# First batch of a fused attention and MLP kernel: lambda spread as three 16-bit rows ahead of q's transposes, alpha1 around pooled k, alpha2 multiplied behind the transposes of u

## The chip, the cores and the metric

The kernel runs on one core of one Trainium2 chip. The metric is the device time of one execution in microseconds (us); the kernel before was timed three times. Its engines are TensorE (PE in the profile; PEld is its weight load), VectorE (DVE), ScalarE (ACT), GpSimd (POOL) and SyncE (SP). Loads and stores are DMA transfers, issued here from the queues of GpSimd, SyncE and ScalarE.

## The reference

Two stages over 8 batches of 576 tokens with 8 heads of 64. First attention with k and v averaged over groups of 8 tokens, so 72 pooled tokens; then a residual MLP with affine vectors:

```python
k_p = k.reshape(B, H, Sp, pool, D).mean(axis=3)
v_p = v.reshape(B, H, Sp, pool, D).mean(axis=3)
scores = scale * np.matmul(q, k_p.transpose(0, 1, 3, 2))
attn = softmax(scores)                       # written out, with + 1e-09
x = attn @ v_p                               # heads side by side: 576 x 512

a1 = alpha1 * x + beta1
tok = np.einsum('ts,bsd->btd', w_tok, a1)    # mixes tokens
u = x + lam * tok
a2 = alpha2 * u + beta2
ch = np.maximum(a2 @ w_ch1, 0.0) @ w_ch2     # 512 -> 2048 -> 512
out = u + lam * ch
```

`lam`, `alpha1` and `alpha2` are vectors of 512 columns.

## The kernel before, in words

**Tiling.** Tokens lie on the 128 partitions, five chunks of them to a batch; the fifth has 64 tokens and is joined with that of the neighbouring batch. Chunks are collected in blocks of four, and the MLP runs on one block of 512 tokens at a time. Block n is computed while the attention of batch n+1 runs between its matmuls. The first batch has no block to hide in: its attention and mix stand alone at the start, and this is the part that is changed.

**Order.** Nothing is scheduled by a planner there: each engine does its instructions in the order in which the Python code issues them (the calls from line 993 on). From block 0 on, the steps are sorted by a due time written beside each (`attention`, line 1076, and the loop at 1127), and are then issued in that order. An engine that waits holds everything behind it. DMA loads are issued in the same order on their engine's queue; those from GpSimd take some 0.6 to 0.9 us of GpSimd each. [...]

**The start.** `keep_warm` (788) runs matmuls on a tile of zeros until q is there. `att_F` (575) transposes q on TensorE, two calls for four heads; `cast_rem` (351) and `att_Frem` (603) do the same for the 64 tokens at the end. `spread_lam` (488) copies the row of lambda to all partitions by a matmul of a row of ones with it, in fp32, and ScalarE evicts it to `lam_bc`. `double_k` (618) repeats a quarter of k on VectorE, for `att_K` (624), which pools k with matmuls and evicts it twice, on ScalarE and on VectorE. `spread_al1` (494) spreads half of alpha1 by an fp32 matmul and multiplies it with `lam_bc` to `lamal_bc`. `att_S` (673) computes the scores of a head and their exponentials, `first_V` (651) pools v, `att_AV` (733) multiplies and normalises, and `att_X` and `rest_X` (761, 754) multiply with `lamal_bc` to `xs`, the moving operand of the mix. PSUM for all this comes from one pool of six banks, in turn.

**The mix.** `setup_wtok` (509) transposes w_tok, `setup_rowsum` (522) sums its rows for beta1 (`bias_row`, 469, is the row that they multiply). `mix_T` (794) computes the mix of one chunk, adds x on VectorE to `u`, and for batch 0 multiplies with `al2_bc`, alpha2 on all partitions, to the 16-bit `u_bf`: on GpSimd for chunks 0 and 2, on VectorE for 1 and 3. `al2_bc` is loaded by `load_al2` (484), 256 KB on SyncE's queue. `mix_uT` (813) transposes `u_bf` on TensorE for block 0, and ScalarE copies the result to `u_fm`, the MLP's moving operand. In later blocks alpha2 is inside w1 (`scale_w1`, 550) and DMA does the transposes.

**Batch 1, beside block 0.** Its q and k are loaded at the start from GpSimd's queue (lines 995 to 998), the w1 pieces 1 and 2 and v and w2 later (1047, 1056, 1060, 1064). `sum_k` (368) adds rows of k on GpSimd before `att_K` pools them; `cast_rem` on GpSimd makes `rem_q` and `rem_k` between the two halves. Both must be done when TensorE comes to `att_K(1, 0)`.

Of the kernel before, what the change touches and what calls it, by code (L numbers as in the profile page):

```python
# [14 lines left out]
P = 128  # L15
# [173 lines left out]
def direct(  # L189
# [199 lines left out]
    al2_bc = const.tile([P, DM], FP, tag="al2_bc", name="al2_bc")  # L389
    b2row = const.tile([8, P], FP, tag="b2row", name="b2row")  # L390

    vecs = const.tile([65, 3, DM], FP, tag="vecs", name="vecs")
# [59 lines left out]
            kpT_pool.append(t)  # L452
            kp_pool.append(const.tile([P, 4, SPG], BF, tag=f"kp_{i}", name=f"kp_{i}"))
    for i in range(2):
        t = const.tile([SPG, 4, S + 64], F16, tag=f"ET_{i}", name=f"ET_{i}")
        nc.vector.memset(t[:, :, S:], 1.0)
        ET_pool.append(t)
    xs_pool = [const.tile([P, 5, DM], BF, tag=f"xs_{i}", name=f"xs_{i}") for i in range(2)]
    nc.vector.memset(xs_pool[1][0:64, 4, :], 0.0)
    nc.vector.memset(pool_v[:, 64:], 0.0)  # L460
    nc.vector.memset(pool_vr, 0.0)
    nc.vector.memset(vr16, 0.0)
# [12 lines left out]
    wtT = const.tile([P, 6, 640], BF, tag="wtT", name="wtT")  # L475
    ones_lo = const.tile([P, P], BF, tag="ones_lo", name="ones_lo")

    def more_constants():
        nc.vector.memset(ones_bf, 1.0)
        nc.vector.memset(ones_lo[0:64], 1.0)  # L480
        nc.vector.memset(ones_lo[64:128], 0.0)
        nc.vector.memset(wtT[:, :, S:640], 0.0)

    def load_al2(behind):
        behind.memset(al2_bc[:, 0:1], 0.0)
        nc.sync.dma_start(out=al2_bc, in_=moe_alpha2.unsqueeze(0).to_broadcast((P, DM)))

    def spread_lam():

        ps = gp("ps_bc")  # L490
        nc.tensor.matmul(out=ps, lhsT=ones_row, rhs=vecs[0:1, 0])
        nc.scalar.copy(out=lam_bc, in_=ps)

    def spread_al1(half):

        ps = gp("ps_bc")[:, 0:256]
        cols = slice(256 * half, 256 * half + 256)
        nc.tensor.matmul(out=ps, lhsT=ones_row, rhs=vecs[0:1, 2, cols])
        nc.vector.tensor_tensor(out=lamal_bc[:, cols], in0=lam_bc[:, cols], in1=ps, op=ALU.mult)

    def setup_vectors():
        ps = gp("ps_vec")
# [115 lines left out]
    def double_k(u):  # L618

        nc.vector.tensor_copy(out=st1[0]["k"][u][:, :, 4], in_=st1[0]["k"][u][:, :, 0])  # L620
        if u == 0:
            cast_rem_k(nc.vector)

    def att_K(b, u, copy):

# [159 lines left out]
            }  # L785
        return key, st2[key]

    def keep_warm(count):

        ps = psB.tile([P, DM], FP, tag="ch", bufs=2, name="ps_warm")  # L790
        for _ in range(count):
            nc.tensor.matmul(out=ps, lhsT=warm[:, 0:P], rhs=warm)  # L792

    def mix_T(b, c, eng=nc.vector):
# [13 lines left out]
        if b:  # L808
            nc.scalar.copy(out=s["u_bf"], in_=s["u"])  # L809
        else:  # L810
            eng.tensor_tensor(out=s["u_bf"], in0=s["u"], in1=al2_bc, op=ALU.mult)

    def mix_uT(key):
        s = st2[key]
        i = where[key]
        blk, at = i // 4, i % 4
        if blk not in u_fm:
            u_fm[blk] = work.tile([P, 4, 512], BF, tag="u_fm", bufs=3, name="u_fm")
        if blk:
            nc.sync.dma_start_transpose(out=u_fm[blk][:, :, 128 * at:128 * at + 128],  # L820
                                        in_=s["u_bf"])
            return
        ps_uT = gp("ps_uT").bitcast(BF)
        for cc in range(4):
            nc.tensor.transpose(out=ps_uT[0:P, 128 * cc:128 * cc + 128],  # L825
                                in_=s["u_bf"][:, 128 * cc:128 * cc + 128], identity=identity_bf)
        nc.scalar.copy(out=u_fm[blk][:, :, at // 2, 128 * (at % 2):128 * (at % 2) + 128],
                       in_=ps_uT[:, 0:512].rearrange("p (c t) -> p c t", t=128))


    H4 = {}
# [78 lines left out]
    def weight_sum(i, g):  # L910
        lo, hi = w2l[g], w2l[g + 2]
        if "T1" not in wino:
            for t, tag in ((1, "w2_2"), (3, "w2_3")):
                wino[f"T{t}"] = const.tile([P, 8, HALF], BF, tag=tag, name="w2_t")
            wino["T2"] = [work.tile([P, 4, HALF], BF, tag="q_bf", bufs=4, name="w2_t2")
                          for _ in range(2)]
            wino["S2"] = [const.tile([P, 4, HALF], BF, tag=tag, name="h_s")
                          for tag in ("early", "al2_bc")]
# [75 lines left out]
    load_w1(0)  # L994
    load_q_bf(1, 0)
    load_q_bf(1, 1)
    for u in range(2):
        load_k(1, u, queue=nc.gpsimd)
    keep_warm(13)
    att_F(0, 0)  # L1000
    att_F(0, 1)
    cast_rem(0, nc.vector)
    more_constants()
    keep_warm(1)
    att_Frem(0, nc.scalar.copy)
    keep_warm(1)
    spread_lam()
    double_k(0)
    att_K(0, 0, None)
    spread_al1(0)  # L1010
    bias_row(0)
    att_S(0, 0)
    att_S(0, 1)
    first_V(0, 0)
    att_S(0, 2)
    double_k(1)
    att_AV(0, 0)
# [7 lines left out]
    att_AV(0, 3)  # L1025
    att_X(0, 2, 4, nc.gpsimd, False)
    rest_X(0, 0, 4, nc.gpsimd)
    att_S(0, 4)
    spread_al1(1)
    late_copy(nc.scalar.copy)  # L1030
    first_V(0, 1)
    load_al2(nc.vector)
    att_S(0, 5)
    att_AV(0, 4)
    att_S(0, 6)
# [8 lines left out]
    setup_wtok(2, nc.scalar.copy)  # L1044
    setup_rowsum(0)
    rest_X(0, 4, 6, nc.gpsimd)
    load_w1(1)
    setup_wtok(3, nc.scalar.copy)
    setup_rowsum(1)
    setup_wtok(4, nc.scalar.copy)  # L1050
    att_X(0, 6, 8)
    bias_row(1)
    mix_T(0, 0, nc.gpsimd)
    setup_vectors()
    setup_rowsum(2)
# [71 lines left out]
    for n in range(NBLK):  # L1127
# [51 lines left out]
                for m in range(4):  # L1179
                    todo.append((27.2 if m < 2 else 29.2, lambda m=m: store(n, m)))  # L1180
        if n == 0:
            todo.append((6.2, lambda: setup_rowsum(4)))
# [68 lines left out]
```

## Time and profile before

| | |
|---|---|
| median of 3 runs | 332.91 us (332.65 to 333.45) |
| the profiled execution | 332.3 us, its span 330.6 |
| TensorE busy | 324.9 us, 98% of the span |
| VectorE, ScalarE, GpSimd | 235.5, 175.5, 95.6 us |
| TensorE starts | 1.39 us |
| q's first transposes in the chain | 7.04 us |
| pooled k of batch 0, first half | 9.09 to 9.77 us |
| first mix matmul | 21.19 us |
| first halves of the MLP end | 29.54 us |
| pooled k of batch 1, first half | 35.36 to 35.52 us |

The page gives busy times per engine. The chain of waits follows the last instruction back to what released it, or to the instruction before it on its engine; read forwards, it says at each moment what the end of the program hung on. A matmul in it that is longer than its like hides a wait. A line of the timeline holds the start, the length, the engine, line, operation and tile, and in brackets how long the engine had been idle and what ended that. Landing times are from the start of a transfer's issue until its data is there.

### The profile page before, as it was taken

Reading aid. Unit: us, or ns where it says so; the run is one execution under the profiler, and the core shown is the slowest. Engines: PE = TensorE matmul, PEld = TensorE weight load, DVE = VectorE, ACT = ScalarE, POOL = GpSimd, SP = SyncE. Lnnn points to the kernel's source line nnn. Section 1 sums busy time; section 2 is a strip of 40 time slices with the busy share of each in tenths; the row PEclk is TensorE's granted clock in tenths of the full one; section 3 lists DMA queues with packets and bytes.
Section 4 is the critical chain, followed back from the end, with each engine's and each line's share of the span. In section 5 each row is a group of like instructions: output and inputs, shape, how many; then the busy total and the mean of one; then the engine's idle time right before and its main releaser. Section 6 shows DMA issues by size and latency. Waiting matters only on the chain.

```text
span 330.6 us, 6522 instructions
## 1 busy us (share of the span) xinstructions
PE 324.9 (98%) x2528; PEld 208.9 (63%) x2528; DVE 235.5 (71%) x490; ACT 175.5 (53%) x322; POOL 95.6 (29%) x110
## 2 busy tenths in 40 slices
PE   8999999999999999999999999999999999999995
PEld 3667764455545576656775677557755866586584
DVE  6674389999589969776967796878688783265263
ACT  2775989458323852387128812782268225803710
POOL 8769738301256011700290028102610200000000
PEclk9999999999999999999999999999999999999999
DMA  8999999959894982499549934995340044003003
GB/s 119 193 219 270 268 210 249 207 145 124 165 255 68 221 203 59 76 227 165 164 119 201 171 125 89 207 195 157 65 136 2 0 65 143 2 0 129 2 32 97
DMA packets 66618, 45.83 MB, mean 139 GB/s; under 512 B 34541, under 2 KB 57205, under 8 KB 66586
## 3 DMA queue, kind: packets, MB, share of 16 engines
q1 hardware_dynamic: 52236, 32.67, 42.6%
q0 software_dynamic: 13824, 12.40, 22.9%
q8 instruction: 20, 0.33, 0.4%
q10 hardware_dynamic: 526, 0.34, 0.3%
q14 instruction: 12, 0.10, 0.1%
HBM read 38.30 MB, written 9.44 MB: 144 GB/s over the span
## 4 chain that ended last, share of the span: by engine, by line
PE 98%; DVE 1%; issue 0%; ACT 0%
PE ps_h L849 38%; PE ps_w L972 26%; PE ps_tok L801 12%; PE ps_ch L869 8%; PE ps_av L743 3%; PE ps_s L700 2%; PE ps_warm L792 2%; PE ps_kp L632 1%; PE ps_r L707 1%; PE ps_av L747 1%; PE ps_q L589 1%; PE ps_sc L680 0%; PE ps_rs L528 0%; PE ps_w L516 0%; PE ps_uT L825 0%; PE ps_v L659 0%
## 5 line engine op out<-in xcount | busy, mean ns | idle before, releaser
L849 PE MATMUL ps_h<-u_fm,w 128*128 128x512 bf16 (+2 forms) x608 | 133.7, 369 | 0.2 <-DVE bias_cols L852 0.2
L856 ACT ACTIVATE H<-ps_h,bias_cols 128x512 bf16<-128x512 f32 x144 | 98.1, 688 | 56.5 <-PE ps_h L849 55.5
L849 PEld LDWEIGHTS <-w 128*128 128x128 bf16 x608 | 65.8, 114 | 49.7 <-issue 2.2
L972 PEld LDWEIGHTS <-H 128*128 128x128 bf16 x560 | 53.4, 98 | 10.9 <-DVE u_sb L990 1.2
L809 ACT CAST u_bf<-u_sb 128x512 bf16<-128x512 f32 x32 | 19.8, 618 | 70.0 <-issue 39.9
L972 PE MATMUL ps_w<-w_l,H 128*128 128x256 bf16 x448 | 53.6, 273 | 0.0
L990 DVE TENSOR_TENSOR u_sb<-u_sb,ps_w 128x512 f32<-128x512 f32 x54 | 36.3, 682 | 17.0 <-PE ps_w L972 17.0
L765 POOL TENSOR_TENSOR xs<-x_tm,lamal_bc 128x512 bf16<-128x512 f32 x12 | 15.9, 1330 | 108.8 <-DVE x_tm L751 108.6
L801 PE MATMUL ps_tok<-xs,wtT 128*128 128x512 bf16 (+3 forms) x200 | 44.9, 381 | 0.1
L805 DVE TENSOR_TENSOR u_sb<-x_tm,ps_tok 128x512 f32<-128x512 f32 (+1 forms) x40 | 27.3, 683 | 9.9 <-PE ps_tok L801 9.9
L751 DVE TENSOR_TENSOR x_tm<-ps_av,recs 128x320 f32<-128x320 f32 x64 | 31.5, 492 | 2.6
L729 ACT ACTIVATE ET<-ps_s 72x512 f16<-72x512 f32 x56 | 32.3, 591 | 0.0
L801 PEld LDWEIGHTS <-wtT 128*128 128x128 bf16 (+3 forms) x200 | 17.4, 100 | 16.2 <-issue 1.1
L749 DVE RECIPROCAL recs<-ps_av 128x5 f32<-128x5 f32 x64 | 12.1, 188 | 16.7 <-PE ps_av L747 16.6
L670 DVE TENSOR_TENSOR v_u<-v_u 72x1024 f32<-72x1024 f32 (+1 forms) x24 | 22.7, 948 | 0.2
L972 PE MATMUL ps_w<-w_t,h_s 128*128 128x256 bf16 x168 | 22.6, 273 | 0.0
L869 PEld LDWEIGHTS <-H 128*128 128x128 bf16 x128 | 11.9, 98 | 13.7 <-issue 0.4
L372 POOL TENSOR_TENSOR k_raw<-k_raw 128x512 f32<-128x512 f32 x14 | 18.7, 1338 | 1.2 <-PE ps_ch L869 0.7
L972 PEld LDWEIGHTS <-h_s 128*128 128x128 bf16 x168 | 16.4, 98 | 4.1
L941 DVE TENSOR_TENSOR H<-H,H 128x1024 bf16<-128x1024 bf16 x14 | 9.7, 690 | 12.8 <-ACT H L856 12.7
L374 POOL TENSOR_TENSOR k_bf<-k_raw 128x512 bf16<-128x512 f32 x14 | 18.5, 1318 | 1.1
L743 PEld LDWEIGHTS <-ET 72*128 72x128 f16 x256 | 14.0, 97 | 6.0 <-DVE vp L664 0.3
(153 smaller groups left out, 369.3 us busy)
## 6 DMA issues: line engine op xcount, KB each, us to landing
out_dram<-u_sb SPq DMA_DIRECT2D x29, 256.0 KB
k_raw<-in_k_dram SPq DMA_DIRECT2D x12, 512.0 KB
v_u<-in_v_dram SPq DMA_DIRECT2D x12, 512.0 KB
q_bf<-in_q_dram POOLq DMA_DIRECT2D x16, 256.0 KB, 7.4
w<-in_moe_w_ch_dram POOLq DMA_DIRECT2D x6, 512.0 KB, 12.9
out_dram<-u_sb SPq DMA_DIRECT2D x11, 128.0 KB
w<-in_moe_w_ch_dram POOLq DMA_DIRECT2D x1, 1024.0 KB, 14.3
k_raw<-in_k_dram POOLq DMA_DIRECT2D x2, 512.0 KB, 16.7
```

The source lines that it names most:

```text
L670: nc.vector.tensor_tensor(out=out, in0=t[:, :, 0:width], in1=t[:, :, width:2 * width], op=ALU.add)
L729: nc.scalar.activation(out=o, in_=i, func=AF.Exp, bias=0.0, scale=0.125)
L743: nc.tensor.matmul(out=av[:, odd + c, :], lhsT=ET[:, m0:m0 + 128], rhs=vp1[:, h % 4, :])
L751: nc.vector.tensor_tensor(out=x[:, 1 - odd:6 - odd, dd:dd + D], in0=av[:, :, 0:64], in1=rec.unsqueeze(2).to_broadcast((P, 5, D)), op=ALU.mult)
L801: nc.tensor.matmul(out=ps_tok[p0:p1], lhsT=wtT[0:kk, at, P * c:P * c + p1 - p0], rhs=xs_pool[i][0:kk, sc, :], start=(sc == 0), stop=(sc == 4))
L805: nc.vector.tensor_tensor(out=s["u"][p0:p1, :], in0=x[p0:p1, 1 + c if c < 4 else 5 - 5 * i, :], in1=ps_tok[p0:p1, 0:DM], op=ALU.add)
L809: nc.scalar.copy(out=s["u_bf"], in_=s["u"])
L849: nc.tensor.matmul(out=ps_h[:, t0:t1 + one], lhsT=w1_of(cc, j), rhs=rhs, start=(cc == 0), stop=(cc == 3))
L856: nc.scalar.activation(out=H4[n, j // 4][:, j % 4, :], in_=ps_h, func=AF.Relu, bias=bias_cols[:, j:j + 1], scale=1.0)
L869: nc.tensor.matmul(out=ps, lhsT=H_of(n, j)[:, 128 * m:128 * m + 128], rhs=(w2l if n else w2)[j // 4][:, j % 4, :], start=(j == 0), stop=(j ...
L972: nc.tensor.matmul(out=ps, lhsT=stat(j), rhs=moving(j), stop=(j == 7), start=(first and (pp == 0 or alone) and j == 0), skip_group_check=True)
L990: nc.vector.tensor_tensor(out=o, in0=o, in1=banks[key, "both"], op=ALU.add)
```

## The change

- `keep_warm` takes a width. The 13 matmuls of 512 columns become 14 of 64 and 8 of 512; the two single ones among q's transposes go.
- Lambda is split on VectorE into three bf16 rows that add up to it (a copy, the rest, a copy of that, the rest again), written into the first rows of `xs_pool[0]`, and spread by three bf16 matmuls ahead of q's transposes. Its eviction comes after the first eviction of pooled k on ScalarE.
- Alpha1's first half is spread ahead of pooled k, its second half right behind it, where it stood behind head 4's scores. Both VectorE products follow the second eviction of pooled k.
- `load_al2` and `al2_bc` go. For batch 0, ScalarE casts `u` to `u_bf`, and VectorE multiplies with alpha2, per partition, as it evicts the transposes.
- VectorE's memsets are put elsewhere: ones_bf before lambda's rows, ET behind `double_k`, the others of `more_constants` behind the alpha1 products, `vr16` behind head 3. `cast_rem_k` stands ahead of `double_k(0)`, `bias_row(0)` behind the first `first_V`.
- `load_w1(1)` is issued ahead of batch 1's k loads on GpSimd's queue. `setup_rowsum(4)` moves from block 0's due times to the end of the first MLP halves, and the first two `mix_uT` each move ahead by one step.

```diff
+    nc.vector.memset(ones_bf, 1.0)
+    rest = const.tile([1, DM], FP, tag="h_s", name="lam_rest")
+    parts = xs_pool[0][0:1, 0:3]
+    nc.vector.tensor_copy(out=parts[:, 0], in_=vecs[0:1, 0])
+    nc.vector.tensor_tensor(out=rest, in0=vecs[0:1, 0], in1=parts[:, 0], op=ALU.subtract)
+    nc.vector.tensor_copy(out=parts[:, 1], in_=rest)
+    nc.vector.tensor_tensor(out=parts[:, 2], in0=rest, in1=parts[:, 1], op=ALU.subtract)
...
+    def fill_ends():
+        for t in ET_pool:
+            nc.vector.memset(t[:, :, S:], 1.0)
+
     def more_constants():
-        nc.vector.memset(ones_bf, 1.0)
+        nc.vector.memset(xs_pool[1][0:64, 4, :], 0.0)
...
-    def load_al2(behind):
-        behind.memset(al2_bc[:, 0:1], 0.0)
-        nc.sync.dma_start(out=al2_bc, in_=moe_alpha2.unsqueeze(0).to_broadcast((P, DM)))
-
     def spread_lam():
         ps = gp("ps_bc")
-        nc.tensor.matmul(out=ps, lhsT=ones_row, rhs=vecs[0:1, 0])
-        nc.scalar.copy(out=lam_bc, in_=ps)
+        for part in range(3):
+            nc.tensor.matmul(out=ps, lhsT=ones_bf[0:1], rhs=xs_pool[0][0:1, part],
+                             start=(part == 0), stop=(part == 2))
+        def finish():
+            nc.scalar.copy(out=lam_bc, in_=ps)
+        return finish
...
+    def cast_u(b, c):
+        s = chunk_of(b, c)[1]
+        nc.scalar.copy(out=s["u_bf"], in_=s["u"])
...
         if b:
-            nc.scalar.copy(out=s["u_bf"], in_=s["u"])
-        else:
-            eng.tensor_tensor(out=s["u_bf"], in0=s["u"], in1=al2_bc, op=ALU.mult)
+            cast_u(b, c)
...
-        nc.scalar.copy(out=u_fm[blk][:, :, at // 2, 128 * (at % 2):128 * (at % 2) + 128],
-                       in_=ps_uT[:, 0:512].rearrange("p (c t) -> p c t", t=128))
+        nc.vector.tensor_tensor(
+            out=u_fm[0][:, :, at // 2, 128 * (at % 2):128 * (at % 2) + 128],
+            in0=ps_uT[:, 0:512].rearrange("p (c t) -> p c t", t=128),
+            in1=al2_cols.unsqueeze(2).to_broadcast((P, 4, 128)), op=ALU.mult)
...
     load_q_bf(1, 1)
+    load_w1(1)
     for u in range(2):
         load_k(1, u, queue=nc.gpsimd)
-    keep_warm(13)
+    keep_warm(14, 64)
+    keep_warm(8)
+    lam_copy = spread_lam()
     att_F(0, 0)
     att_F(0, 1)
     cast_rem(0, nc.vector)
-    more_constants()
-    keep_warm(1)
-    att_Frem(0, nc.scalar.copy)
-    keep_warm(1)
-    spread_lam()
-    double_k(0)
-    att_K(0, 0, None)
-    spread_al1(0)
-    bias_row(0)
+    cast_rem_k(nc.vector)
+    att_Frem(0, nc.scalar.copy)
+    al1_copies = [spread_al1(0)]
+    double_k(0)
+    fill_ends()
+    att_K(0, 0, None)
+    lam_copy()
+    al1_copies.append(spread_al1(1))
+    for copy in al1_copies:
+        copy()
+    more_constants()
     att_S(0, 0)
     att_S(0, 1)
     first_V(0, 0)
+    bias_row(0)
...
-    spread_al1(1)
     late_copy(nc.scalar.copy)
     first_V(0, 1)
-    load_al2(nc.vector)
...
-    load_w1(1)
...
-    mix_T(0, 0, nc.gpsimd)
+    mix_T(0, 0)
     setup_vectors()
+    cast_u(0, 0)
     setup_rowsum(2)
     load_w1(2)
     mix_T(0, 1)
+    mix_uT((0, 0))
+    cast_u(0, 1)
     setup_rowsum(3)
-    mix_T(0, 2, nc.gpsimd)
+    mix_T(0, 2)
     load_v32(1)
-    mix_uT((0, 0))
     mix_uT((0, 1))
+    cast_u(0, 2)
     mix_T(0, 3)
+    cast_u(0, 3)
...
     mlp_A(0, 3, 0, 256)
+    setup_rowsum(4)
     for j in range(4):
         mlp_A(0, j, 256, 512)
```

More of the change, by code (lines that the diff above doesn't have):

```diff
@@ L388, in direct @@
     lamal_bc = const.tile([P, DM], FP, tag="lamal_bc", name="lamal_bc")
-    al2_bc = const.tile([P, DM], FP, tag="al2_bc", name="al2_bc")
     b2row = const.tile([8, P], FP, tag="b2row", name="b2row")
@@ L454, in direct @@
     for i in range(2):
-        t = const.tile([SPG, 4, S + 64], F16, tag=f"ET_{i}", name=f"ET_{i}")
-        nc.vector.memset(t[:, :, S:], 1.0)
-        ET_pool.append(t)
+        ET_pool.append(const.tile([SPG, 4, S + 64], F16, tag=f"ET_{i}", name=f"ET_{i}"))
     xs_pool = [const.tile([P, 5, DM], BF, tag=f"xs_{i}", name=f"xs_{i}") for i in range(2)]
-    nc.vector.memset(xs_pool[1][0:64, 4, :], 0.0)
     nc.vector.memset(pool_v[:, 64:], 0.0)
     nc.vector.memset(pool_vr, 0.0)
-    nc.vector.memset(vr16, 0.0)
+    nc.vector.memset(ones_bf, 1.0)
[5 more added lines that the diff above has]
+    nc.vector.tensor_tensor(out=parts[:, 2], in0=rest, in1=parts[:, 1], op=ALU.subtract)
     nc.vector.tensor_scalar(out=pool_v[:, 0:64], in0=pool_main, scalar1=8.0, scalar2=None,
@@ L498, in spread_al1, with finish @@
         nc.tensor.matmul(out=ps, lhsT=ones_row, rhs=vecs[0:1, 2, cols])
-        nc.vector.tensor_tensor(out=lamal_bc[:, cols], in0=lam_bc[:, cols], in1=ps, op=ALU.mult)
+        def finish():
+            nc.vector.tensor_tensor(out=lamal_bc[:, cols], in0=lam_bc[:, cols], in1=ps,
+                                    op=ALU.mult)
+        return finish
     def setup_vectors():
@@ L620, in double_k @@
         nc.vector.tensor_copy(out=st1[0]["k"][u][:, :, 4], in_=st1[0]["k"][u][:, :, 0])
-        if u == 0:
-            cast_rem_k(nc.vector)
     def att_K(b, u, copy):
@@ L786, in chunk_of, with keep_warm, mix_T @@
         return key, st2[key]
-    def keep_warm(count):
-        ps = psB.tile([P, DM], FP, tag="ch", bufs=2, name="ps_warm")
+    def keep_warm(count, n=DM):
+        ps = psB.tile([P, DM], FP, tag="ch", bufs=2, name="ps_warm")[:, 0:n]
         for _ in range(count):
-            nc.tensor.matmul(out=ps, lhsT=warm[:, 0:P], rhs=warm)
-    def mix_T(b, c, eng=nc.vector):
+            nc.tensor.matmul(out=ps, lhsT=warm[:, 0:P], rhs=warm[:, 0:n])
+    def cast_u(b, c):
+        s = chunk_of(b, c)[1]
+        nc.scalar.copy(out=s["u_bf"], in_=s["u"])
+    def mix_T(b, c):
         key, s = chunk_of(b, c)
@@ L917, in weight_sum @@
             wino["S2"] = [const.tile([P, 4, HALF], BF, tag=tag, name="h_s")
-                          for tag in ("early", "al2_bc")]
+                          for tag in ("early", "h_s")]
             wino["S3"] = [const.tile([P, 4, HALF], BF, tag="lam_bc", name="h_s"),
@@ L1027, in direct @@
     rest_X(0, 0, 4, nc.gpsimd)
+    nc.vector.memset(vr16, 0.0)
     att_S(0, 4)
-    spread_al1(1)
     late_copy(nc.scalar.copy)
     first_V(0, 1)
-    load_al2(nc.vector)
     att_S(0, 5)
@@ L1181, in direct @@
         if n == 0:
-            todo.append((6.2, lambda: setup_rowsum(4)))
             todo.append((8.3, setup_wtok_odd))
```

## The prediction

> **What bounds the kernel now.** I read the busy table of the page first, then the chain of waits in order of time over the first 80 us, then POOL's timeline, and last the landing times of single transfers. The busy table says that TensorE is the bound; its idle time is 5.7 us of 330.6.
>
> ```profile
> PE 324.9 (98%) x2528; PEld 208.9 (63%) x2528; DVE 235.5 (71%) x490; ACT 175.5 (53%) x322; POOL 95.6 (29%) x110
> ```
>
> So time is won only by taking work off TensorE's own stream, or by shortening one of the few places where it waits, and it is kept only if nothing further down that stream waits for something else. In the chain (start, length, engine, tile, line) the places that the change touches are these:
>
> ```profile
> 1.39 5.66 PE ps_warm L792 x13
> ...
> 8.04 1.05 PE ps_bc L491 x2
> ...
> 9.79 0.40 ACT kpT L648
> ...
> 10.21 0.47 DVE kpT L648
> ...
> 15.31 0.62 PE ps_bc L498 x2
> ...
> 35.36 0.12 PE ps_kp L632 x4
> 35.48 0.04 PE ps_kp L638 x2
> ```
>
> Here are lambda's spread (1.05 us on TensorE), the wait of the first scores for two evictions of pooled k, the second half of alpha1 (0.62), and, 20 us later, batch 1's pooled k, which needs GpSimd's sums. POOL's timeline shows those sums and the loads in front of them:
>
> ```profile
> 12.55 0.76 POOL L280 DMA_DIRECT2D k_raw<-in_k_dram  x1 [0.85 <-PE ps_sc L680]
> 14.24 0.75 POOL L280 DMA_DIRECT2D k_raw<-in_k_dram  x1 [0.93 <-PE ps_kp L638]
> ...
> 30.12 1.33 POOL L372 TENSOR_TENSOR k_raw<-k_raw 128x512 f32<-128x512 f32 x1
> 31.52 1.27 POOL L374 TENSOR_TENSOR k_bf<-k_raw 128x512 bf16<-128x512 f32 x1
> 32.74 0.40 POOL L357 CAST rem_q<-rem_raw 128x256 bf16<-128x256 f32 x1
> 33.10 0.72 POOL L360 TENSOR_TENSOR rem_k<-rem_raw 128x256 bf16<-128x256 f32 x1
> ```
>
> From the first sum to the end of rem_k is 33.82 - 30.12 = 3.70 us, and TensorE uses rem_k at 35.48: 1.66 us of slack. The load that the first sum reads was issued at 12.55 and took
>
> ```profile
> DMA to landing us min/median/max: 16.7/16.7/16.7
> ```
>
> so it landed at 29.25, already after q's second half for batch 1 (issued 10.9, 16.8 to landing: 27.7). The loads of GpSimd's queue land one behind the other in the order of their issue: k's second half at 30.8, then w1's second piece, issued at 21.30, with
>
> ```profile
> DMA to landing us min/median/max: 12.0/12.0/12.0
> ```
>
> at 33.3. That is 2.46 us behind its forerunner; the third piece follows at 35.9, 2.6 later.
>
> **The start, up to q's transposes.** Removed are 13 wide warm-up matmuls, 5.66 us from 1.39, that is 0.427 each. In come 14 of 64 columns, 8 wide ones and lambda's three 16-bit rows. The eleven wide ones at 0.427 are 4.70. A 64-column matmul is not in the trace at this early pace; pooled k's 64-column ones take 0.47/16 = 0.029 later, where a wide one takes 0.22, so 0.06 at the half pace. The other end is the early weight load of 0.15. I take 0.06, the nearer kind: 14 x 0.06 + 4.70 = 5.5, the same as before; with 0.15 it is 1.2 later, and TensorE passes the gate below at 35.6 for 35.48, 0.1 slower. VectorE must have the third row ready by then: a copy and a subtraction, twice, on one row. The bias row (1x512) took 0.68, a 256-wide cast 0.31, a 128-wide one 0.21, so a 512-wide cast about 0.5, the chain 2.4 us. With the ET, xs and vr16 memsets moved away (0.55 + 0.27 + 0.27, the first of them into VectorE's wait for pooled k near 8.3) it starts at 3.7 and ends near 6.1, while the third row is wanted at 6.4. [...] So q's transposes start where they did, about 7.0, and pool_v on VectorE, which ended at 6.14, a little later, with rem_q near 6.5 to 7.0: cost nothing as long as rem_q is there at 7.4.
>
> **From there to the first scores.** Gone are two wide matmuls (0.44) and lambda's 1.05; alpha1's first half (0.62) moves ahead of pooled k. Pooled k ended at 9.77. Now k's landing (2.27 + 5.5 = 7.77) and its doubling (0.23) allow a start near 8.05, and with 0.57 + 0.10 it ends at 8.72: 1.05 earlier. Alpha1's second half now follows it (0.62), under the 0.40 + 0.47 of the two evictions. Lambda's copy (0.58) is behind the first eviction on ScalarE, so the first exponential waits for it, to 9.75. Second half of the first scores: 9.69 instead of 10.73.
>
> **To the mix.** VectorE becomes the limit: after the eviction it has both alpha1 products (0.42 each, from 9.77), the late memsets (about 0.85) and then vp's cast, which ends at 11.9 instead of 12.63. The bias row's 0.68 now stands between that cast and k's second doubling, so the second q copy, which gates the scores of head 4, gains only 0.23 (14.55 for 14.78). But 0.62 of alpha1 is gone behind head 4, and the next vp ends at 16.4 instead of 17.28: 0.9 us. Landing times allow it: q's second half 13.25, v's 14.7, w_tok 17.4, all ahead of their new uses. [...]
>
> **The mix.** ScalarE's four copies of transposed u (0.53 to 0.58) become VectorE products, priced at 0.68 as the like product with PSUM at line 875; two VectorE and two GpSimd products (0.69 to 0.77, 1.26) become ScalarE casts at 0.62 each. Per chunk the path is 0.69 + 0.62 in place of 0.69 + 1.26, and the 0.17 that the transposes waited for GpSimd goes. Against that the first MLP matmul waits about 0.1 for its product, and the second halves 0.25 for the last one, hidden partly by the moved row sum (0.15). Sum at the second halves: 0.95; with the row sum gone from 34.77, 1.1 us ahead when TensorE comes to batch 1's pooled k, at 34.3 instead of 35.36.
>
> **Where it goes.** There the queue order counts. w1's second piece now stands ahead of both k loads in GpSimd's queue, so k's first half lands 2.46 later, at 31.7, less what the removed alpha2 load gives back. That load is 256 KB on SP's queue; the queue view from 20 to 23.7 shows SP's and ScalarE's packets at 21.1% of the engines' time, 0.78 us. At most that comes back, at least nothing. The row nearest to it says little: w1's first piece, under whose transfer it lay, took 23.68 - 18.45 = 5.23, and two later halves 2.46 + 2.6 = 5.06, so 0.17. I take 0.3, near that row. [...]
>
> So k lands at 31.4, GpSimd starts at 31.45, ends rem_k at 35.15, and TensorE passes at 35.2, having stood for 0.8 us. Before, it passed at 35.48. The gain is 0.3 us, between 0.75 and nothing. The second half follows w2's issue (0.57) and two sums (1.3 each) and is ready at 38.4, ahead of its use at 39.2. v lands at 39.8 or earlier, as before, since the queue up to it holds the same loads; w2's loads stay behind it. Nothing later is touched, and TensorE is full from there.
>
> The profiled execution took 332.3, the median of the three runs is 332.91, 0.6 above it. 332.3 - 0.3 = 332.0, and on the scale of the median 332.6.
>
> **The rivals.** *The gain is kept.* If k's first half lands by 30.5 (or GpSimd's four steps take less than their 3.70), TensorE never stands, and 1.1 comes through: 331.8. For it: 98% TensorE, and the alpha2 load's removal. Against it: 2.46 of landing distance is three times what that removal can return.
>
> *The sums come later than I say.* Should w1's piece need more than 2.76 us in its new place, where the remainder rows share the engines (41% of SP's share from 23.7 to 25.6), TensorE passes later than before; with 1 us more than that, 333.6. For it: q's halves in that stretch took 1.9 and 2.1, and 1.3 earlier in the queue. Against it: the remainder rows are over when k passes now, and total traffic falls.
>
> *The slow start lasts longer: slower.* The early wide matmuls step at 0.427, the later ones at 0.22, although the granted clock prints 1.00 throughout; the pace changes near 6.9. If 14 narrow matmuls and three one-row ones do not count as work, it changes later. From 7.0 to the first scores there are about 2.7 us of TensorE work that would double, less 0.4 of waiting that hides it: TensorE is 2.3 later, of which the 1.1 of lead absorbs part, so it passes the gate at 36.7 for 35.48, 1.2 slower: 334.1. It decides from 1.1 us of delay on. Against it: TensorE has no gap from 1.39 on, and lambda's one-row matmuls at 8.04 did not bring the slow pace back. [...]
>
> **How the numbers follow.** The gate at k: 0.62. Gain kept: 0.14. Sums later: 0.12. Slow start: 0.12. A measurement here tells about 0.3%, 1.0 us, from no change. The kept gain is only just over that: with the gate's best end, faster is 0.16. The slow start and half of the late sums: slower 0.17. Same: 0.67. The range runs from 331.7, the kept gain, to 333.9, close to the slow start.
>
> **What would show it.** Right: q's transposes start within 0.2 us of 7.0; the first scores about 1 us earlier; the first mix matmul about 0.9 earlier than 21.19; k's first half lands near 31.4; GpSimd's first sum waits for that load; and TensorE has a gap of 0.5 to 1 us at batch 1's pooled k near 34.4, which is not there now. Wrong: no gap there, or a first sum near 30.1, or q's transposes at the slow pace (over 0.1 us each).

## The result and the profile after

The changed kernel takes 335.13 us (median of 17 executions, 333.76 to 337.04) against 332.9 before; the ratio is 1.0076 with a 95% interval of 1.0056 to 1.0096. It is slower by 2.2 us, and outside the forecast range (331.7 to 333.9). The executions are not spread evenly: 3 lie at 333.8 to 334.1, 7 at 334.9 to 335.3, 2 at 336.0 and 5 at 337.0. This spread is taken up below; where another kernel's executions fall into groups I give the groups, since the ratios leave out those more than 1.5% above the fastest of their kernel.

The profiled execution is one of the slowest group: 337.0 us, span 334.9. Its busy row still has TensorE at 98%, but 4.5 us more of it than before:

```profile
PE 329.4 (98%) x2536; PEld 213.6 (64%) x2536; DVE 238.6 (71%) x495; ACT 175.9 (53%) x322; POOL 93.5 (28%) x108
```

The chain of waits in order of time (start, length, engine, tile, line), at the places that answer to those shown of before:

```profile
1.39 4.34 PE ps_warm L804 x22
5.73 1.39 PE ps_bc L495 x3
7.12 0.97 PE ps_q L603 x8
...
8.30 1.15 PE ps_bc L507 x2
9.44 0.97 PE ps_kp L644 x16
...
10.50 1.15 PE ps_bc L507 x2
...
23.02 0.22 PE ps_av L755 x4
...
25.63 1.24 PE ps_tok L817 x5
...
34.17 1.92 PE ps_h L865 x16
...
39.62 0.12 PE ps_kp L644 x4
```

q's transposes start at 7.12, where the forecast had 7.0. But their eight take 0.97 us, 0.121 each, where they took 0.45 before. Pooled k takes 0.97 for 0.57, and half of alpha1 1.15 for 0.62. I call the slower pace half pace, the faster one full pace. TensorE does everything at half pace until about 23.5: at 23.02 four of `att_AV`'s matmuls still take 0.22 (0.15 at full pace), and the mix that follows has its old 1.24. The first mix is at 25.63 instead of 21.19, and from there nothing is lost or won: 8.54 us to the second halves of the MLP for 8.56 before, and 39.62 for 35.36 at batch 1's pooled k. The 4.3 us of difference in the span (334.9 for 330.6) are all there at the first mix.

This time the granted clock is no help. It prints 1.00 in every stretch of the first 40 us, also where a transpose takes 0.121 for the 0.056 of before; the half pace is read from the length of like instructions.

POOL's timeline (start, length, line, operation, idle time before it and what ended that), at the loads and sums of batch 1:

```profile
13.67 0.76 POOL L280 DMA_DIRECT2D k_raw<-in_k_dram  x1 [0.64 <-DVE wtT L489]
17.10 0.75 POOL L280 DMA_DIRECT2D k_raw<-in_k_dram  x1 [2.67 <-DVE x_tm L763]
...
29.70 1.26 POOL L372 TENSOR_TENSOR k_raw<-k_raw 128x512 f32<-128x512 f32 x1 [1.86 <-DMA k_raw<-in_k_dram]
...
34.58 0.73 POOL L360 TENSOR_TENSOR rem_k<-rem_raw 128x256 bf16<-128x256 f32 x1 [1.93 <-DMA rem_raw<-in_k_dram]
```

The sums wait for k's landing, as forecast, though k lands near 29.6 here and not near 31.4, with the remainder rows loaded later (rem_k waits 1.93 for them). rem_k is done at 35.31, 4.3 us before TensorE comes. The gap forecast at batch 1's pooled k does not exist in this execution: the gate was opened long before.

VectorE's timeline at the start shows two things that matter below: the row chain of lambda ends at 5.75, as forecast (6.1), and the casts of rem_k wait 0.60 us for a transfer, with `double_k`'s copy of k behind them:

```profile
5.07 0.68 DVE L464 TENSOR_TENSOR xs<-lam_rest,xs 1x512 bf16<-1x512 f32 x1
6.19 0.54 DVE L466 TENSOR_SCALAR pool_v<-pool_main 128x64 bf16<-128x64 bf16 x1 [0.44 <-POOL pool_main L434]
...
7.04 0.49 DVE L357 CAST rem_q<-rem_raw 128x256 bf16<-128x256 f32 x1
8.14 0.29 DVE L365 CAST rem_k<-rem_raw 128x256 bf16<-128x256 f32 x1 [0.60 <-DMA rem_raw<-in_k_dram]
8.35 0.22 DVE L366 CAST rem_k<-rem_raw 128x128 bf16<-128x128 f32 x1
8.48 0.50 DVE L634 COPY k<-k 128x256 bf16<-128x256 bf16 x1
```

### The profile page after: what moved, and what is told of

Its sections match the earlier page's. It is cut to its first block, busy times and chain, and to the rows that moved or that the text cites. A ratio compares the mean times of both kernels' runs of the same rounds, so it can differ in the third digit from the quotient of the medians.

```text
span 334.9 us, 6535 instructions
## 1 busy us (share of the span) xinstructions
PE 329.4 (98%) x2536; PEld 213.6 (64%) x2536; DVE 238.6 (71%) x495; ACT 175.9 (53%) x322; POOL 93.5 (28%) x108
## 4 chain that ended last, share of the span: by engine, by line
PE 97%; DVE 1%; issue 0%
PE ps_h L865 38%; PE ps_w L988 26%; PE ps_tok L817 11%; PE ps_ch L885 8%; PE ps_av L755 3%; PE ps_s L712 2%; PE ps_warm L804 1%; PE ps_sc L692 1%; PE ps_kp L644 1%; PE ps_q L603 1%; PE ps_bc L507 1%; PE ps_r L719 1%; PE ps_av L759 1%; PE ps_v L671 1%; PE ps_bc L495 0%; PE ps_v L673 0%
## 5 line engine op out<-in xcount | busy, mean ns | idle before, releaser
L808 ACT CAST u_bf<-u_sb 128x512 bf16<-128x512 f32 x36 | 22.3, 618 | 72.4 <-issue 39.6
L763 DVE TENSOR_TENSOR x_tm<-ps_av,recs 128x320 f32<-128x320 f32 x64 | 31.4, 491 | 2.6
L374 POOL TENSOR_TENSOR k_bf<-k_raw 128x512 bf16<-128x512 f32 x14 | 18.4, 1318 | 1.1
L755 PEld LDWEIGHTS <-ET 72*128 72x128 f16 x256 | 14.9, 102 | 5.5 <-DVE vp L676 0.2
```

The source lines that it names most:

```text
L755: nc.tensor.matmul(out=av[:, odd + c, :], lhsT=ET[:, m0:m0 + 128], rhs=vp1[:, h % 4, :])
L763: nc.vector.tensor_tensor(out=x[:, 1 - odd:6 - odd, dd:dd + D], in0=av[:, :, 0:64], in1=rec.unsqueeze(2).to_broadcast((P, 5, D)), op=ALU.mult)
```

## The experiments

**First question: which of the new matmuls keeps TensorE at half pace?** My theory is that work on one row does not raise the pace (rival "The slow start lasts longer" of the prediction); its rival blames the 14 narrow ones.

The changed kernel with wide matmuls only ahead of lambda's rows:

```diff
-    keep_warm(14, 64)
-    keep_warm(8)
+    keep_warm(10)
```

> The changed kernel with 10 wide warm-up matmuls in place of 14 narrow and 8 wide: lambda's three one-row matmuls start at the same 5.66 us. If the narrow matmuls keep TensorE at the slow pace (theory N), the start is as in the kernel before: q's eight transposes take 0.45 us instead of 0.97 and the time is 331.8 to 332.9. If the one-row matmuls do it (theory R), because they count as no work and only 4.27 us of full work precede them, the slow pace stays past 10 us as in the changed kernel and the time is spread over 334 to 337, median near 335.

Measured: 335.32 (334.51 to 335.93), ratio 1.0071 [1.0047, 1.0095], no better than the change. In its PE timeline lambda's rows and q's transposes are as slow as in the change:

```profile
5.78 1.46 PE L495 MATMUL ps_bc<-xs,ones_bf 1*128 1x512 bf16 x3
7.16 1.03 PE L603 MATMUL ps_q<-identity_bf,q_bf 128*128 128x128 bf16 x8
```

The narrow ones are not to blame. Put into the kernel before, they do no harm:

```diff
-    keep_warm(13)
+    keep_warm(14, 64)
+    keep_warm(11)
```

> The kernel before with 14 narrow and 11 wide warm-up matmuls in place of 13 wide, nothing else changed; q's transposes start at the same 7.0 us. Theory N: the slow pace lasts past 10 us and the time goes to 334 to 337. Theory R: as the kernel before, 332.4 to 333.5, since 4.70 us of wide matmuls stand unbroken ahead of the transposes.

Measured: 332.49 (332.05 to 333.21), ratio 0.9992 [0.9969, 1.0015]. The 25 took 5.60 us, so a narrow one took (5.60 - 11 x 0.427) / 14 = 0.065, for the 0.06 that I had taken.

One-row matmuls put into the kernel before, in place of its last three wide ones:

```diff
-    keep_warm(13)
+    keep_warm(10)
+    keep_warm(3, 1)       # lhsT=warm[0:1, 0:P], rhs=warm[0:1]
```

> The kernel before with the last 3 of its 13 wide warm-up matmuls on one row instead of 128 (zeros as before), nothing else changed. Theory R: the slow pace lasts past 10 us in most executions and the time goes to 334 to 337. Theory N: as the kernel before, 332.4 to 333.5.

Measured: 5 executions at 332.35 to 332.99, 7 at 336.61 to 338.07 (ratio 1.0056 [1.0012, 1.01]). The profile kept is of a quick execution (332.50): its warm-up takes 5.52 us for 5.66, with no gap. Nothing but the rows differs in the code, and 7 of 12 executions lose some 4 to 5 us. No long one was profiled, but five of the seven have mean granted clocks of 0.998 to 1.000, which with such a time points to a late rise and no fall behind it, as in the profile of the change (0.999). The kernel before lost as much by itself in 4 of the 35 executions measured beside it (336.5 to 337.7), but at 0.979 to 0.980, so there the pace fell after it had risen.

Lambda's three rows given 128 partitions, 127 of them zeros:

```diff
+    nc.vector.memset(xs_pool[0][:, 0:3], 0.0)
+    first_row = const.tile([P, P], BF, ...)   # ones in row 0, else zeros
-            nc.tensor.matmul(out=ps, lhsT=ones_bf[0:1], rhs=xs_pool[0][0:1, part],
+            nc.tensor.matmul(out=ps, lhsT=first_row, rhs=xs_pool[0][:, part],
```

> The changed kernel with lambda's three matmuls spread over all 128 rows (zeros in 127 of them, both in the weights and in the moving rows; VectorE clears those rows first, some 0.8 us more on it), the narrow matmuls kept. Theory R (one-row matmuls count as no work): the slow pace ends near 7 us and the time is 331.8 to 333.2. Theory N (the narrow ones are at fault): as the changed kernel, 334 to 337.

Measured: 334.12 (333.86 to 335.0), ratio 1.0037 [1.0007, 1.0066]. Half of the loss is gone: q's eight transposes are back at full pace (0.61 where the wide warm-up alone had 1.03).

```profile
7.15 0.61 PE L607 MATMUL ps_q<-identity_bf,q_bf 128*128 128x128 bf16 x8
```

Rows taken away slow the start (7 of 12 executions), and rows given back restore it (0.61 for 1.03): this shows the cause of the slow start. But then the pace falls. Stretches of two us, with the busy time of each engine (TensorE's second, after the length) and, third from the end, the granted clock:

```profile
9.00:11.00 2.00, 2.00 (x25) 1.25 (x25) 1.21 (x4) 1.04 (x3) 2.00 (x4) 0.83 1.08 134
11.00:13.00 2.00, 2.00 (x11) 1.26 (x9) 1.26 (x6) 1.24 (x4) 2.00 (x4) 0.50 1.29 163
...
17.00:19.00 2.00, 1.79 (x18) 1.16 (x15) 1.82 (x6) 1.53 (x5) 1.72 (x2) 0.96 1.12 210
```

TensorE also stands 0.48 us for rem_q here, since VectorE is later by its zeros. So there is a second question: what makes the pace fall back from about 10.3 to 17.1?

**Second question: the two single wide matmuls that the change removed, and lambda's place.** The kernel before without them:

```diff
-    keep_warm(1)
     att_Frem(0, nc.scalar.copy)
-    keep_warm(1)
```

> The kernel before without its two single wide matmuls beside q's remainder transposes, nothing else changed. Theory K (the stretch after the start must hold enough full-row work too, and the two matmuls, 0.44 us, were part of it): the granted clock shows 0.50 in windows between 10 and 17 us, as it did with lambda on 128 rows, and the time is 334 to 336. Theory S (only the work ahead of q's transposes counts): the pace stays, and the time is 332.2 to 332.8, the 0.44 at most won.

Measured: 332.89 (332.04 to 333.6), ratio 0.9987 [0.9956, 1.0019]. By its times and mean granted clocks (0.997 to 1.000) it keeps its pace in all 10 executions; the expectation that it needs them is not borne out. The changed kernel with them put back:

```diff
+    keep_warm(1)
     att_Frem(0, nc.scalar.copy)
+    keep_warm(1)
```

> The changed kernel with the two single wide matmuls put back around q's remainder transposes. Theory K together with R (lambda's one-row matmuls do not count as work): the start is still slow in most executions, 333.5 to 336. If the two matmuls were all that is missing: 331.8 to 332.6.

Measured: 335.22; two executions at 332.29 and 332.69, the others at 334.31 to 336.89; ratio 1.0067 [1.002, 1.0113]. Eight of the ten stay long: four at 334.31 to 335.25 with mean granted clocks of 0.984 to 0.989, four at 336.45 to 336.89 with 1.000. Its profile (334.31) keeps full pace up to 11.1 and so shows what the change does to pooled k at full pace, in the chain:

```profile
2.62 5.42 DMA rem_raw<-in_k_dram
8.13 0.29 DVE rem_k L365
8.43 0.14 DVE rem_k L366
8.56 0.44 DVE k L634
9.04 0.55 PE ps_kp L644 x13
```

Pooled k ends at 9.70, as before (9.77), and not at 8.72: VectorE holds the copy of k behind the casts of rem_k, whose rows land at 8.04.

Lambda's three 16-bit rows behind q's transposes, with the old 13 wide ones:

```diff
-    keep_warm(14, 64)
-    keep_warm(8)
-    lam_copy = spread_lam()
+    keep_warm(13)
...
     att_Frem(0, nc.scalar.copy)
+    lam_copy = spread_lam()
```

> The changed kernel with 13 wide warm-up matmuls as before and lambda's three rows behind q's remainder transposes, without the two single matmuls. Theory R alone (the one-row matmuls ahead of the transposes were the fault): full pace from 7 us on, 331.5 to 332.4. Theory K: full pace from 7 us, half pace again from about 10.3 on for one or two stretches of 3.4 us, 333 to 335.

Measured: 4 executions at 332.88 to 333.77, 6 at 334.15 to 334.39; ratio 1.0011 [0.9971, 1.0051]. The pace rises as before and falls back in at least five of the six (mean granted clock 0.988 to 0.990; the sixth prints 1.000). The stretches of its profile, columns as above:

```profile
7.00:9.00 2.00, 1.82 (x16) 0.94 (x13) 1.20 (x5) 1.35 (x3) 2.00 (x4) 1.00 1.49 202
9.00:11.00 2.00, 2.00 (x26) 1.32 (x26) 1.35 (x5) 0.96 (x3) 2.00 (x4) 0.78 1.39 182
11.00:13.00 2.00, 2.00 (x11) 1.21 (x9) 1.20 (x6) 1.30 (x4) 2.00 (x3) 0.50 1.26 170
```

TensorE was busy for 3.82 of the 4 us in which this happens. The same with the two wide ones kept:

> As the last, with the two single wide matmuls put back around q's remainder transposes: both causes undone, all else of the change kept. R and K together: full pace from 7 us on, no 0.50 in the granted clock, the first mix matmul 0.5 to 1 us ahead of that of the kernel before, and 331.5 to 332.6. If something else in the change slows the start (one-row alpha1 and the loss of the wide matmuls' like in the stretch), still 333 to 335.

Measured: 332.86; 6 executions at 332.60 to 332.95, 2 at 333.5 to 333.8, 2 at 334.5; ratio 1.0009 [0.9975, 1.0043]. Its profile (332.74, span 330.6, like before's) keeps full pace throughout, and the chain runs through the forecast gate:

```profile
9.28 0.57 PE ps_kp L644 x16
...
13.39 18.08 DMA k_raw<-in_k_dram
...
31.55 1.27 POOL k_raw L372
...
34.51 0.69 POOL rem_k L360
35.20 0.05 issue
35.25 0.21 PE ps_kp L650 x2
```

k's first half lands at 31.47 (forecast 31.4), rem_k ends at 35.20 (35.15), TensorE passes at 35.25 (35.2) having stood for 0.2 us. The lead expected at the first mix is not there: 21.08 for 21.19.

**Third: the queue alone, the gate alone, and another try at the fall.** The kernel before with `load_w1(1)` alone moved ahead of batch 1's k loads:

```diff
     load_q_bf(1, 1)
+    load_w1(1)
     for u in range(2):
         load_k(1, u, queue=nc.gpsimd)
...
     rest_X(0, 4, 6, nc.gpsimd)
-    load_w1(1)
```

> The kernel before, with one line moved: w1's second piece is issued ahead of batch 1's k loads on GpSimd's queue, as in the changed kernel; the alpha2 load stays. It prices the queue order alone. By step (Where it goes): k's first half lands 2.46 later than its 29.25, near 31.7, GpSimd's first sum waits for it, rem_k ends near 35.4 and TensorE, which comes to it at 35.3, passes about 0.1 to 0.2 later: the time is that of before within 0.3 us (332.7), because before's own slack of 1.66 us hid the old landing and 0.7 of the new one at most shows. If removing the alpha2 load gave nothing back, k lands here where it landed with the lambda rows behind and the wide matmuls kept (31.5); if it gave back all 0.78, it lands near 32.2 and TensorE stands 0.6 longer (333.3).

Measured: 333.29 (332.44 to 334.35), ratio 1.0014 [1.0004, 1.0025]. k's first half, issued at 13.09, lands 18.4 later at 31.49, as POOL's timeline shows at the first sum:

```profile
31.57 1.27 POOL L372 TENSOR_TENSOR k_raw<-k_raw 128x512 f32<-128x512 f32 x1 [2.00 <-DMA k_raw<-in_k_dram]
```

PE's timeline has TensorE standing for rem_k (idle time in brackets):

```profile
35.28 0.22 PE L638 MATMUL ps_kp<-pool_rem,rem_k 128*128 128x16 bf16 x2 [0.37 <-POOL rem_k L360]
```

It stands 0.37 us, and the medians differ by 0.4. The two need not be the same: in this execution the warm-up was shorter (5.03 for 5.66), TensorE came early, and it passes rem_k at 35.28, where the kernel before passed it at 35.31 by the same timeline. With the alpha2 load in place k lands at 31.49, without it (lambda behind, the wide ones kept) at 31.47. That does not price the load, since the two kernels differ in more: without it GpSimd issues its loads some 0.6 us later (w1's first piece at 9.96 for 9.37), and q's second half, ahead of w1's second piece in the queue, lands 0.9 earlier all the same (26.6 for 27.5).

The kernel with lambda behind and the wide ones kept, with `load_w1(1)` in its old place (the reverse of the diff above):

> The changed kernel with 13 wide matmuls, lambda's rows behind q's remainder transposes with a wide matmul on either side of these, and w1's second piece back in its old place behind the first batch's products on GpSimd. Against the same kernel without the last step this takes the k gate alone away: k's first half should land near 29, GpSimd's first sum start by 30.2 and TensorE not stand at batch 1's pooled k, where it stood 0.3 us (34.95 to 35.25). Expected 0.2 to 0.4 us below that kernel's quick executions (332.6 to 332.95): 332.3 to 332.6. If the k gate was no limit, the time is the same, 332.8.

Measured: 333.01; 8 executions at 332.43 to 333.12, 4 at 334.0 to 334.5; ratio 1.0007 [0.9984, 1.0029]. k lands at 28.7, again by POOL's timeline at the first sum:

```profile
28.82 1.27 POOL L372 TENSOR_TENSOR k_raw<-k_raw 128x512 f32<-128x512 f32 x1 [1.20 <-DMA k_raw<-in_k_dram]
```

In PE's timeline the same matmul as above has no idle time before it:

```profile
35.02 0.21 PE L650 MATMUL ps_kp<-pool_rem,rem_k 128*128 128x16 bf16 x2
```

This k lands some 0.5 ahead of the 29.25 of the kernel before, which has the alpha2 load and the same queue order; here too GpSimd's loads are issued 0.6 later. TensorE passes 0.23 earlier, and its last matmul of the program ends 0.24 earlier (326.70 for 326.94). The time does not show it: what follows that matmul varies by 0.5 us between these two profiles. The expected 332.3 to 332.6 is a miss, within what can be told.

For the fall of the pace I tried taking one-row work out, alpha1's second half back behind head 4's scores:

```diff
-    al1_copies.append(spread_al1(1))
...
     att_S(0, 4)
+    spread_al1(1)()
```

> The changed kernel with 13 wide matmuls, lambda's rows behind q's remainder transposes, no single wide matmuls, and alpha1's second half spread where the kernel before had it, behind head 4's scores. In the stretch from 7.0 to 10.4 us this takes 0.62 us of one-row matmuls out and lets 0.6 us more of scores and pooled v with 72 to 128 rows in; the wait for rem_q (0.2 us) stays. If the share of one-row matmuls in a stretch decides whether the pace holds, it holds here as in the kernel before without its two single wide matmuls: no 0.50 in the granted clock from 10 to 18 us, and at most 2 of 10 executions above 333.5. If the wait for rem_q, or the lack of wide matmuls as such, made it fall, 5 or more of 10 are at 334 as in the same kernel with alpha1's second half early.

Measured: 335.52; one execution at 333.57, six at 334.36 to 338.72; ratio 1.0069 [1.0037, 1.0101]. It got no better, so one-row work is not the whole of it. The stretches of its profile, columns as above:

```profile
7.00:9.00 2.00, 1.62 (x12) 0.74 (x9) 1.18 (x5) 1.35 (x3) 2.00 (x4) 1.00 1.45 201
9.00:11.00 2.00, 1.48 (x22) 1.09 (x21) 1.05 (x4) 0.87 (x2) 2.00 (x4) 0.54 1.38 178
```

TensorE is now busy for only 3.10 of these 4 us: it stands 0.38 for rem_q, and without alpha1's second half it stands 0.48 while pooled k is evicted. Only the first can have to do with the fall: a mean of 0.54 from 9 to 11 puts the fall at 9.17, and the second begins at 10.06. The same with `load_w1(1)` in its old place:

> As the kernel with alpha1's second half late, and w1's second piece back in its old place on GpSimd's queue: both causes undone, the slow pace and the k gate. By the share of one-row matmuls and the k gate: TensorE comes to batch 1's pooled k by 34.9 and does not stand there; 332.0 to 332.5 in most executions, 0.2 to 0.4 below the kernel before of the same chip. If the pace falls all the same: 334.

Measured: 334.49; 6 executions at 333.07 to 334.0, 6 at 335.0 to 338.45; ratio 1.0035 [1.0009, 1.006]. The same groups, so no more can be read from it.

**Last: standing or one-row work?** Both added one at a time to the kernel that kept its pace in all 10 executions, the one before without its two single wide ones. (Those 10 were on another chip; the kernel before behaved alike on both, with 3 of 30 and 2 of 26 executions above 336.)

```diff
-    cast_rem(0, nc.vector)
     more_constants()
+    cast_rem(0, nc.vector)
```

> The kernel before without its two single wide matmuls (which kept its pace in all of 10 executions), with VectorE's memsets of more_constants (0.67 us) ahead of the cast of rem_q instead of behind it: TensorE stands about 0.4 to 0.6 us at q's remainder transposes near 7.3, and the one-row work is the same. If standing makes the pace fall back: 3 or more of 10 executions at 334 or above with a mean granted clock of 0.990 or less. If one-row matmuls do it: none, and the time is 332.9 plus at most the 0.6 of standing.

Measured: all 4 executions long, 334.61 to 337.53, with mean granted clocks of 0.979 to 0.990; ratio 1.01 [1.0068, 1.0132]. TensorE stood for 0.35 us, and the pace fell at 10.2 for 6.8 us; PE's timeline and one stretch:

```profile
7.80 0.28 PE L613 MATMUL ps_qr<-identity_bf,rem_q 128*128 128x128 bf16 x2 [0.35 <-DVE rem_q L357]
...
11.00:13.00 2.00, 2.00 (x11) 1.25 (x9) 0.85 (x2) 1.34 (x4) 1.22 (x2) 0.50 1.45 199
```

```diff
     spread_al1(0)
+    spread_al1(1)
...
     att_S(0, 4)
-    spread_al1(1)
```

> The kernel before without its two single wide matmuls, with alpha1's second half spread right behind the first: 0.62 us more of one-row matmuls in the stretch from 7 to 10.4 us, no more standing than before (0.1). If one-row matmuls make the pace fall back: 3 or more of 10 executions at 334 or above with a mean granted clock of 0.990 or less. If standing does it: none, 332.5 to 333.5.

Measured: 3 executions at 332.45 to 332.81, 7 at 334.05 to 334.37; ratio 1.0018 [0.9993, 1.0042]. In its profile (332.81, a quick one) TensorE has no gap at all in the stretch and the pace falls all the same, for 3.4 us (10.8 to 14.2); the stretches:

```profile
7.00:9.00 2.00, 2.00 (x18) 1.14 (x17) 1.33 (x7) 1.39 (x4) 2.00 (x4) 1.00 1.47 204
9.00:11.00 2.00, 2.00 (x28) 1.58 (x26) 0.92 (x3) 1.03 (x3) 2.00 (x4) 0.95 1.46 192
11.00:13.00 2.00, 2.00 (x12) 1.12 (x10) 0.97 (x2) 1.20 (x4) 1.46 (x2) 0.50 1.45 199
13.00:15.00 2.00, 2.00 (x37) 1.88 (x37) 1.59 (x6) 1.43 (x4) 0.00 (x0) 0.69 1.15 227
15.00:17.00 2.00, 2.00 (x34) 1.53 (x30) 1.86 (x6) 1.57 (x5) 1.61 (x2) 1.00 1.05 197
```

Either was enough: 0.35 us of standing in the stretch behind the rise (all 4 executions long), or 0.62 of one-row matmuls there (7 of 10), and the kernel before without its two wide ones no longer held the pace that it had held in all 10 executions.

At last the change with both taken out: lambda's rows on 128 partitions, VectorE's memsets of `vp` and the second `kpT` moved behind the alpha1 products to pay for the zeros, and the two single wide ones:

```diff
+    nc.vector.memset(xs_pool[0][:, 0:3], 0.0)      # and first_row, as above
-            nc.vector.memset(t, 8.0)               # vp, now in more_constants
...
+    keep_warm(1)
     att_Frem(0, nc.scalar.copy)
+    keep_warm(1)
```

> The changed kernel with lambda's three rows spread from 128 partitions (127 of them zero), four memsets of VectorE (1.1 us: vp, the second kpT) moved behind the alpha1 products to pay for the zeros, and a wide matmul on either side of q's remainder transposes. All of the change stays: lambda ahead of q, alpha1 around pooled k, alpha2 on VectorE, the queue order. If the pace is all of the loss: pooled k ends by 9.2, the first mix is at 20.6 or earlier, TensorE stands 0.3 to 0.9 at batch 1's pooled k and passes it near 35.2, and most executions take 332.3 to 332.8. If something else of the change costs time: 333.5 or more at full pace.

Measured: 333.52; 7 executions at 332.72 to 333.57, 5 at 333.75 to 334.73; ratio 1.0018 [1.0005, 1.0032]. The groups above 335 are gone. But at full pace the first mix is at 21.80, behind before's 21.19, most likely because the memsets that I moved make VectorE late (vp's cast ends at 13.33 for 12.63 before, and TensorE waits 0.93 for it); so this kernel can't show what the front half is worth. The same with `load_w1(1)` in its old place:

> As the kernel with full rows, and w1's second piece back in its old place on GpSimd's queue: k's first half lands near 29, TensorE does not stand at batch 1's pooled k and passes it at 34.2 to 34.7 instead of 35.2. 331.6 to 332.2 in most executions, 0.5 to 1.0 below the kernel before. If the front half's gain is not there, it equals the kernel with full rows, 332.5.

Measured: 334.08 (332.78 to 335.61), ratio 1.0021 [0.999, 1.0053]: a miss, for the same reason, and the pace fell back at 11.5 in its profile. No version of the change is quicker than the kernel before.

## Why the prediction was wrong, step by step

**The start.** The start time was right: 7.12 for 7.0, a narrow matmul 0.065 for 0.06, the row chain done at 5.75 for 6.1. (The 0.427 is the step from one wide matmul to the next; 5.66 / 13 is 0.435, since the last one's end counts in too.) The words that failed are "cost nothing": they price lambda's rows ahead of q by their length alone. They filled the last 1.4 us of the warm-up with one-row work, and the transposes behind it took 0.121 each for 0.056. The three one-row matmuls in the kernel before (7 of 12 executions long) and lambda's rows on 128 partitions (the eight transposes at 0.61 for 1.03) show the cause from both sides. So the rival "The slow start lasts longer" is what happened, by its one-row part alone; I gave it 0.12. Its price was low too: it had half pace only up to the first scores, 2.7 us of work, and cost 1.2 net. That the slow pace ends there no run shows: the profiled execution has it to 23.5 and loses 4.3 (2.2 by the medians). What keeps the pace down so long is open: from 11.65 to 22.4 no one-row matmul runs in that profile and TensorE has no gap, yet the pace does not rise. Matmuls on 72 or 32 rows, with 72 columns of weights, or of only 64 or 66 columns fill much of that stretch; whether these keep it down was not tried. The argument that I put against it, that lambda's one-row matmuls at 8.04 do no harm in the kernel before, was a reading of one point: the kernel before without its two wide ones kept its pace beside them in all 10 executions, and with 0.62 us more of one-row spreads it had 3.42 us of half pace in its profile and 7 of 10 executions at 334.05 to 334.37.

**To the first scores.** 1.05 us were forecast. At full pace the trace has none of it: pooled k ends at 9.70 for the 8.72 of the forecast. I let it start from k's landing (7.77) and its copy, and did not price `cast_rem_k`, which I had named as moved ahead of `double_k`: it waits on VectorE for rem_k's rows (8.04), with the copy queued behind. Beside that, rem_q was late (7.53 for 6.5 to 7.0), because GpSimd's select that pool_v waits for took 0.69 where it took 0.24 before. The move back of `cast_rem_k` alone was not tried.

**To the mix, and the mix.** The 0.9 at the first mix was nowhere seen: 21.08 for 21.19 with lambda behind q's transposes. That kernel has lambda and the two wide matmuls back in the path, so it does not test all of the 0.9. From the first mix to the second halves, 0.05 were forecast (0.95 after 0.9), and 0.02 measured, in the changed kernel too (25.63 to 34.17). The products at 0.69 and the casts at 0.62 are as priced. The row sum's 0.15 came: 5.45 from the second halves to batch 1's pooled k (34.17 to 39.62) for 5.61.

**Where it goes.** The wait for k is as forecast, the gain is not. In the kernel with lambda behind q and full pace, k's landing, rem_k's end and TensorE's passing came within 0.07 of the forecast, but TensorE stood for 0.2 and not 0.8, since it came at 34.9 to 35.0 and not at 34.3. Its median, 332.86, is that of the kernel before beside it (332.85): that this is near the forecast 332.6 is no support for the gain of 0.3. The landing is in part luck. The queue order alone moved it by 2.2 us (29.25 to 31.49) and not 2.46. What the alpha2 load gave back no run isolates: nothing by 31.47 for 31.49, some 0.5 by 28.7 for 29.25, and the 0.3 of the forecast lies between. The other end of the forecast, all 0.78 given back and a gain of 0.75, was my estimate from the queue view (21.1% of 20 to 23.7), and no run shows it: the 0.9 by which q's second half landed earlier speaks for it, k's landing at the same time against it. In the changed kernel none of this is reached, since TensorE comes 4 us late.

**The length of the falls.** Where the granted clock shows a fall, the pace stayed at half for 6.82 to 6.83 us in five of the traces, 3.42 in one and 17.06 in one: two, one and five times 3.41. The rise came at different moments: the same 13 wide matmuls took 5.66 us in the profile of before and 4.76 in that of the kernel with lambda behind, the wide ones kept and w1's piece in its old place. Whether this makes the groups of times is open; one profile to a kernel can't show it. The pace fell with TensorE busy for 3.82 and 4.00 of the 4 us around the fall, so being busy was not enough. How much full-row work holds the pace stays open too: in the profile of the kernel with alpha1's second half late TensorE was busy for 2.94 of the 3.41 us ahead of the fall (5.76 to 9.17), yet that of the same kernel with w1's piece back kept its pace with 2.79 busy of the 4 us from 7 to 11.

## What to carry to other kernels

A matmul moved into TensorE's warm-up, or into the first few us behind it, has to be priced by its rows as well as by its length: here 0.62 us of one-row spreads made the pace fall, as 0.35 us of standing did. A start that holds its pace in every execution is not thereby safe; the one here was 0.35 us of standing, or 0.62 of one-row work, from one that does not hold it, so look at how the times of a changed kernel group, not at one profile. And when a step is moved ahead of another on an engine, ask what it waits for before you count the time that the other wins.

## What the runs showed of the hardware that I had not expected

- Matmuls with one row did not do for TensorE's pace what full ones did: three in place of the last three of 13 wide ones cost some 4 to 5 us in 7 of 12 executions.
- The pace fell back from full to half with no gap on TensorE: 10.8 to 14.2 us in the trace with alpha1's second half early, at 2.00 busy of each 2.00 us.
- The granted clock printed 1.00 in the first 40 us of the changed kernel, also where like matmuls took twice their time (0.121 for 0.056 a transpose); in the falls of other kernels it printed 0.50.
- A GpSimd select beside VectorE's lambda chain took 0.69 us for 0.24.
- 256 KB taken off one queue did not bring the transfers on another forward alike: in one pair of kernels q's second half landed 0.9 us earlier (26.6 for 27.5) and k, two transfers behind it, at the same time (31.47 for 31.49). Other transfers had moved too, so the reason is open.
